# Two products of the second unit woven among the first unit's at the head of a Strassen-style gated layer

## The chip, the cores and the metric

The kernel runs on one core of a Trainium2 chip. The metric is the device time of one execution in microseconds (us); the time given is the median of the runs shown.

## The reference, cut to what matters

Causal attention, then a layer with a rational activation ("layer 1"), then a gated layer ("layer 2"), each on the output of the one before:

```python
x = attention(q, k, v)                       # 2 x 12 heads, 448 x 64 -> x is 896 x 768
h = x @ w_in                                 # 768 -> 2048
g = (a0 + a1*h + a2*h**2 + a3*h**3) / (1 + |b0|*|h| + |b1|*h**2 + 1e-6)
x = g @ w_out                                # 2048 -> 768
gate = 1 / (1 + exp(-(x @ w_gate)))          # 768 -> 1536
out = (gate * (x @ w_val)) @ w_out2          # 1536 -> 768, out is 896 x 768
```

The weights come as 64-bit floats and are unpacked on the chip. Every operand of a matrix product is kept as a pair hi, lo of two rounded numbers, and a product is three matmuls: hi by hi, hi by lo, lo by hi.

## The kernel before, in words

**Layer 1** works in four chunks (c = 0 to 3) of four 128-column tiles of `w_in`. The tokens come in two blocks (b = 0, 1); after the first chunk these are 384 and 512 tokens wide. For each chunk and block a stage "in" makes the tiles h and passes each through `rational` (lines 276 to 307: three ACT instructions L289 to L291, three of DVE L293 to L295, two of ACT L298 and L299, three of DVE L301 to L303, an ACT copy L305 to the hi half and a POOL subtraction L307 to the lo half), and a stage "out" multiplies by `w_out` in six column tiles e of four steps i each (matmuls L336 to L338). Each out tile is summed on DVE (L348); in the last chunk its result is rounded to xh (ACT L354) and xl (POOL L357).

**Layer 2** works in twelve units u. A unit makes the gate and the value product for 128 columns from seven products (`PRODUCTS`, a table of weights, activations and the PSUM accumulator A to D): p1 opens A, p6 opens B, p7 opens C, p5 opens D; p2, p4 and p3 add to A, C and D once these have been read. Each product is three steps of three matmuls (`product`, L475 to L477), nine in all. The sums of activations t1, t3, t2, t4 are made once, on DVE (`act_sum`, L448 to L454), rounded on ACT (L460) and their lo halves made on POOL, that of t3 on DVE (L464). `combine` (L480 to L512) reads the accumulators: "p1" is an ACT copy of A to x (L488), "u2" adds B to x (DVE L490), "u3" adds C and gives y (DVE L492), "c22" adds D to y (L494), "sg1" is the sigmoid of A (ACT L496), and so on to the halves gh and gl (ACT L510, POOL L512).

p2 can begin only after "p1" has read A, p4 only after "u3" has read C, and p3 only after "c22" has read D.

**The weights of a unit** come in two portions q (`weight2`): two DMAs each into a buffer `raw` (L402, two such buffers, shared with the portions of `w_out` and `w_out2`), two ACT instructions (L407, L409), one of DVE (L412). `weight_sums` makes s1 to s4 on DVE (L426 to L430) into the `raw` buffer of the second portion. Then each product's weights are copied to a slot's hi half by ACT (L436) and the lo half is subtracted on POOL (L440). There are ten slots; slots 8 and 9 lie in the second room of SBUF (room_b), the others in room_a. Unit u's product number n takes slot (7u + n) mod 10 and waits for the last matmul of the product that had the slot.

**The order** of each engine's instructions is fixed when the program is built. `stage_in`, `stage_out`, `unit_of_weights` and `stage_out2` write PE's order out by hand. Everything else is a job with an engine, a cost, its dependencies and a rank; `in_turn` (L35) takes on each engine, of the jobs that are ready by those costs, the one with the lowest rank. A rank is a place on PE's own line of costs plus an offset from the table `R`: "e" for DVE and POOL jobs of `combine`, "p1" for its ACT jobs, "ts", "th" and "tl" for the sums of activations, "w2" for unpacking a unit's weights, "wh" for its sums and halves, "sum" for what follows an out tile, in every chunk and in the output stage.

**The PSUM banks:** ring b has four banks and holds a unit's A to D (line 471); rings a and d have two each and hold the last six tiles of layer 1 and the tiles z of the output stage (`place`, line 925).

PE's order around the change is: the last out stage of layer 1; unit 0 as p1, p5, p2, p7, p6, p4, p3; units 1 and 2 each as p1, p6, p7, p5, p2, p4, p3; then the first group of the output stage (z, L529 to L531) over units 0 and 1, units 3 and 4, and so on.

Of the kernel before, what the change touches and what calls it, by code (L numbers as in the profile page):

```python
# [71 lines left out]
def tile_causal_attention__moe_rational__moe_glu(  # L72
# [349 lines left out]
    def weight_sums(u, k):  # L422
# [5 lines left out]
        else:  # L428
            nc.vector.tensor_tensor(a["s3"], a["a11"], a["a21"], op=ALU.subtract)
            nc.vector.tensor_tensor(a["s4"], a["a12"], a["s2"], op=ALU.subtract)  # L430

    def slot(u, name):
        return store["w"][(len(PRODUCTS) * u + list(PRODUCTS).index(name)) % NW]

    def weight_hi(u, name):
        nc.scalar.copy(slot(u, name)[0], halves[u, PRODUCTS[name][0]])  # L436
# [29 lines left out]
    def product(u, name, c):  # L466

        w, x, b, opens = PRODUCTS[name]
        if name == "p1" and c == 0:
            for k in "ABCD":  # L470
                unit_ps[u, k] = bank["b"].tile([P, 512], F32, tag="mm", name=f"u{u}_{k}")[:, :S]
        ps = unit_ps[u, b]
        (hi, lo), (bh, bl) = slot(u, name), act[x]
        begins, ends = opens and c == 0, c == KH - 1
        nc.tensor.matmul(ps, hi[:, c], bh[:, c], start=begins, stop=False, skip_group_check=True)  # L475
        nc.tensor.matmul(ps, hi[:, c], bl[:, c], start=False, stop=False, skip_group_check=True)  # L476
        nc.tensor.matmul(ps, lo[:, c], bh[:, c], start=False, stop=ends, skip_group_check=True)  # L477
# [239 lines left out]
    J = {}  # L717
# [12 lines left out]

    NG = len(GROUPS)
    LA = 2
    R = dict(last=0.0, rat0=-985.0, rat1=0.0, rl=4.0, s=-37.5, turn=-18.0, r=-8.0, row=-2.0, x=34.0, w=-3.0, max=-17.0, copy=-9.5, inv=1.0, xn=-0.5, rout=-4.0, exp=6.25, hi=18.0, lo=4.5, e=-8.0, p1=18.0, ts=-8.0, th=-7.0, tl=-6.5, wh=2.0, w2=-8.5, sum=-1.0)
    C = dict(w_at=11.0, row=0.1, o_at=37.98, o_step=3.0, w_step=5.5, s=0.28, p=0.1, x=0.15, max=0.08, exp=0.19, switch=0.05, stay=11.0, copy=0.0, wa=0.1, wd=0.26, xn=0.13, rat=0.16, inv=0.15)
    H = dict(PE=0.17, DVE=0.13, ACT=0.17, POOL=0.12, SP=0.03)
    MODES = {"s": "rows", "p": "rows", "x": "columns", "r": "rows"}
    EXP = (0.39, 0.48, 0.57, 0.67)
# [135 lines left out]
    def weights_in2(u):  # L873
# [10 lines left out]
        for k in range(2):  # L884
            deps = [("w2", u, 0, 3), ("w2", u, 1, 3)] + [("ws", u, 0)] * k
            job(("ws", u, k), "DVE", 1.1, deps, (("P", u, "p6", 0), R["wh"]), weight_sums, u, k)
        for i, name in enumerate(PRODUCTS):
            n = len(PRODUCTS) * u + i
            if n >= NW:
                free = [last_of((n - NW) // len(PRODUCTS), list(PRODUCTS)[(n - NW) % len(PRODUCTS)])]  # L890
# [36 lines left out]
    def place(key, read):  # L927

        after = key[:3] != ("in", 0, 0) and (key[:3] != ("in", 0, 1) or key[3] >= EARLY)
        n_tiles[after] += 1  # L930
        if key[:3] == ("out", NCH - 1, 1) or key[0] == "out2":
            n_tiles[2] += 1
            r = "ad"[n_tiles[2] // 2 % 2]
        else:
            r = "b" if after and (n_tiles[1] - 1) % 6 < 4 else "a"
        deps = freed_by(r, 4 if r == "b" else 2) + ["late"] * after
        freed[r].append([(*key, "after", read)])
        ring[key] = r
        return deps

# [70 lines left out]
        "gl2": ("POOL", 1.11, [], ["gh2"]),  # L1011
    }

    def unit_of_weights(u, order):

        nonlocal unit
        for name in order:
            deps = [("wl", u, name)]
            if not u and PRODUCTS[name][3]:
                deps += freed_by("b", 4 - "ABCD".index(PRODUCTS[name][2]))  # L1020
            deps += [("e", u, {"p2": "p1", "p4": "u3", "p3": "c22"}[name])] if name in ("p2", "p4", "p3") else []
            if u and PRODUCTS[name][3]:
                deps.append(("e", u - 1, {"A": "sg1", "B": "u2", "C": "pr1", "D": "pr2"}[PRODUCTS[name][2]]))
            for c in range(KH):
                x = PRODUCTS[name][1]
# [10 lines left out]
            for what, (engine, cost, after, others) in AFTER.items():  # L1036
# [2 lines left out]
                deps_e = [("P", u, n, KH - 1) for n in after] + [("e", u, o) for o in others]  # L1039
                if what == "p1" and u > 1:  # L1040
                    deps_e += [("e", u - 2, "c12"), ("e", u - 2, "gl1")]
                if what == "sg1":
                    deps_e += [("in", NCH - 1, 1, NF - 1, "after", 2)]
                    deps_e += [("e", u - 1, "c12")] if u else []
# [5 lines left out]
                if what == "gh2" and u < NG2 or what == "gh1" and u < NG2:  # L1050
                    deps_e.append(("out", NCH - 1, 1, KC - 1, "mm", NF - 1))
                job(("e", u, what), engine, cost, deps_e, at["end"] + R["p1" if engine == "ACT" else "e"], combine, u, what)

    def sums_of_x():

# [63 lines left out]
        _run(stage_out(*ins[n - 1]))  # L1119
    _run(stage_out(*ins[-1]))  # L1120
    sums_of_x()
    unit_of_weights(0, ("p1", "p5", "p2", "p7", "p6", "p4", "p3"))
    unit_of_weights(1, PRODUCTS)
    unit_of_weights(2, PRODUCTS)
    u = 3
    for group in range(len(GROUPS2)):
        _run(stage_out2(group))
        for _ in range(2):
            if u < NU and u < 2 * group + 5:
                unit_of_weights(u, PRODUCTS)  # L1130
                u += 1
    for j in J.values():
        if isinstance(j.rank, tuple):
            j.rank = at[j.rank[0]] + j.rank[1] if isinstance(j.rank[0], tuple) else at[j.rank]

    latest = {}
    for j in in_turn(J, {**H, "": 0.0}, C["switch"], C["stay"]):
# [59 lines left out]
```

## Time and profile before

| | |
|---|---|
| median of 3 runs | 577.6 us (577.32 to 578.62) |
| profiled execution, its own time | 580.54 us |
| its span | 577.5 us |
| time around the span | 3.04 us |
| PE busy | 559.4 us, 97% of the span, 3388 matmuls |
| DVE, ACT, POOL busy | 433.2, 383.4, 334.3 us |
| granted TensorE clock, mean | 0.997 |

A row of a timeline gives the start and the length of an instruction or of several alike (xN), and in brackets how long the engine had been idle and what ended that. Matmuls overlap: the pace is the distance of their starts, not their length. "SPq" is the queue from which the loads are issued.

### The profile page before, as it was taken

To read this page: it belongs to the slowest core of one execution; us is meant where nothing else is said; L and a number is where in the kernel's file an instruction comes from. 1 tells how busy PE (TensorE), PEld (TensorE's weight loads), DVE (VectorE), ACT (ScalarE), POOL (GpSimd) and SP (SyncE) were. 2 spreads that over 40 slices of the span, in tenths; PEclk is the share of its full clock that TensorE was granted. 3 is DMA by queue.
4 is the path that set the end of the run, shared out by engine and by line. 5 is a ranking of instruction groups with operands and counts; after the bars stand their busy time and mean duration, and the time that the engine had idled before them with its cause. 6 is when DMAs were issued, how large, how long until landed. Compare 5 with 4: busy or idle time off the path is not lost.

```text
span 577.5 us, 9390 instructions
## 1 busy us (share of the span) xinstructions
PE 559.4 (97%) x3388; PEld 486.0 (84%) x3388; DVE 433.2 (75%) x802; ACT 383.4 (66%) x767; POOL 334.3 (58%) x284
## 2 busy tenths in 40 slices
PE   7898999999999999999999989999999999999997
PEld 4455666699988988898888879999999999999996
DVE  5788899877758986899579877527876976757557
ACT  6799898788869494859285557577646466547210
POOL 1557544385377457445647987558647746665510
PEclk9899999999999999999999999999999999999999
DMA  8357540153154243304230103434244234432105
GB/s 278 106 186 239 178 137 18 33 187 102 63 171 158 65 155 102 117 0 132 88 111 0 56 0 110 165 110 149 71 165 140 69 120 165 126 129 76 53 0 192
DMA packets 35247, 65.29 MB, mean 113 GB/s; under 512 B 2369, under 2 KB 22593, under 8 KB 35201
## 3 DMA queue, kind: packets, MB, share of 16 engines
q1 hardware_dynamic: 35200, 64.70, 33.6%
q8 instruction: 26, 0.43, 0.3%
q14 instruction: 21, 0.16, 0.1%
HBM read 61.93 MB, written 2.75 MB: 112 GB/s over the span
## 4 chain that ended last, share of the span: by engine, by line
PE 83%; DVE 10%; POOL 2%; ACT 2%; DMA 1%; issue 1%; SPq 1%; DVEq 0%; POOLq 0%; ACTq 0%
PE h L274 7%; PE h L275 6%; PE h L276 6%; PE o L337 6%; PE o L338 6%; PE o L336 6%; PE z L529 5%; PE z L530 4%; PE z L531 4%; PE x L677 3%; PE s L595 3%; PE u_C L475 3%; PE u_C L477 3%; PE u_C L476 3%; PE u_A L475 2%; PE u_A L477 2%
## 5 line engine op out<-in xcount | busy, mean ns | idle before, releaser
L189 POOL TENSOR_TENSOR ol_out<-val_out,oh_out 128x768 fp32r<-128x768 f32 x28 | 55.2, 1971 | 10.9 <-ACT oh_out L187 9.5
L440 POOL TENSOR_TENSOR room_a<-val,room_a 128x384 fp32r<-128x384 f32 x30 | 32.5, 1091 | 42.3 <-ACT room_a L436 42.2
L529 PE MATMUL z<-oh_out,room_b 128*128 128x384 f32 (+2 forms) x168 | 56.6, 337 | 0.3 <-DVE y L539 0.3
L530 PE MATMUL z<-ol_out,room_b 128*128 128x384 f32 (+2 forms) x168 | 56.3, 335 | 0.0
L531 PE MATMUL z<-oh_out,room_b 128*128 128x384 f32 (+2 forms) x168 | 56.2, 335 | 0.0
L539 DVE TENSOR_TENSOR y<-y,z 128x384 f32<-128x384 f32 (+1 forms) x84 | 43.8, 550 | 12.6 <-PE z L531 12.4
L617 ACT ACTIVATE e<-e,sc 120x224 f32<-120x224 f32 (+3 forms) x96 | 49.8, 524 | 4.6 <-DVE sc L603 4.5
L440 POOL TENSOR_TENSOR room_a<-raw,room_a 128x384 fp32r<-128x384 f32 x38 | 45.8, 1221 | 8.4 <-ACT room_a L436 8.4
L603 DVE CUSTOM_DVE_ANT_0 e<-s,mask 120x224 f32<-120x224 f32 (+3 forms) x96 | 38.0, 444 | 14.1 <-PE s L595 14.0
L177 DVE SCALAR_TENSOR_TENSOR val_out<-raw_out 128x768 uint32<-128x768 uint32 x28 | 35.7, 1276 | 16.6 <-ACT raw_out L174 10.3
L307 POOL TENSOR_TENSOR room_a<-t_h,room_a 128x384 fp32r<-128x384 f32 (+1 forms) x16 | 17.9, 1121 | 48.8 <-ACT room_a L305 48.6
L307 POOL TENSOR_TENSOR room_b<-t_h,room_b 128x512 fp32r<-128x512 f32 (+1 forms) x16 | 21.7, 1357 | 36.5 <-ACT room_b L305 36.5
L595 PE MATMUL s<-qk 64*120 64x224 f32 (+3 forms) x192 | 32.3, 437 | 6.2 <-DVE sc L603 6.2
L337 PE MATMUL o<-room_b,oh_out 128*128 128x512 f32 (+1 forms) x96 | 37.0, 386 | 1.0 <-POOL room_b L307 1.0
L274 PE MATMUL h<-xh,room_a 128*128 128x448 f32 (+2 forms) x96 | 36.9, 384 | 0.7 <-DVE t_h L295 0.7
L338 PE MATMUL o<-room_b,ol_out 128*128 128x512 f32 (+1 forms) x96 | 36.9, 385 | 0.0
L336 PE MATMUL o<-room_b,oh_out 128*128 128x512 f32 (+1 forms) x96 | 36.8, 384 | 0.0
L289 ACT ACTIVATE z_h<-h 128x384 f32<-128x384 f32 (+2 forms) x32 | 17.5, 548 | 26.5 <-PE h L276 26.5
L275 PE MATMUL h<-xl,room_a 128*128 128x448 f32 (+2 forms) x96 | 35.0, 364 | 0.0
L276 PE MATMUL h<-xh,room_a 128*128 128x448 f32 (+2 forms) x96 | 34.9, 363 | 0.0
L275 PE MATMUL h<-xl,room_b 128*128 128x384 f32 (+1 forms) x96 | 34.7, 362 | 0.0
L412 DVE SCALAR_TENSOR_TENSOR val<-raw 128x768 uint32<-128x768 uint32 x24 | 24.3, 1013 | 13.9 <-ACT raw L409 13.8
(179 smaller groups left out, 1866.8 us busy)
## 6 DMA issues: line engine op xcount, KB each, us to landing
raw_out<-in_moe_w_out_dram SPq DMA_DIRECT2D x28, 768.0 KB, 4.2
raw_in<-in_moe_w_in_dram SPq DMA_DIRECT2D x16, 768.0 KB, 4.9
raw<-in_moe_w_gate_dram SPq DMA_DIRECT2D x24, 384.0 KB, 3.3
raw<-in_moe_w_val_dram SPq DMA_DIRECT2D x24, 384.0 KB, 3.9
qk<-in_qk_dram SPq DMA_DIRECT2D x12, 464.0 KB, 5.5
v<-in_v_dram SPq DMA_DIRECT2D x12, 224.0 KB, 3.4
out_dram<-y SPq DMA_DIRECT2D x14, 192.0 KB, 2.4
a_sb<-in_moe_a_dram SPq DMA_DIRECT2D x1, 2.0 KB, 6.8
```

The lines of the kernel that those rows point to most:

```text
L189: nc.gpsimd.tensor_tensor(lo, vf, hi, op=ALU.subtract)
L274: nc.tensor.matmul(ps, hi[:, c, fs], xh[:, c, bs], start=(c == 0), stop=False)
L275: nc.tensor.matmul(ps, hi[:, c, fs], xl[:, c, bs], start=False, stop=False)
L276: nc.tensor.matmul(ps, lo[:, c, fs], xh[:, c, bs], start=False, stop=(c == KC - 1))
L336: nc.tensor.matmul(ps, hi[:, es], gh, start=(i == 0), stop=False)
L337: nc.tensor.matmul(ps, hi[:, es], gl, start=False, stop=False)
L338: nc.tensor.matmul(ps, lo[:, es], gh, start=False, stop=(i == NF - 1))
L440: nc.gpsimd.tensor_tensor(lo, halves[u, PRODUCTS[name][0]], hi, op=ALU.subtract)
L529: nc.tensor.matmul(ps, gh[:, ms], hi[:, ns], start=(u == us[0]), stop=False)
L530: nc.tensor.matmul(ps, gh[:, ms], lo[:, ns], start=False, stop=False)
L531: nc.tensor.matmul(ps, gl[:, ms], hi[:, ns], start=False, stop=(u == us[-1]))
L617: nc.scalar.activation(e, e, AF.Exp, bias=d["sc"][:, t, j : j + 1], scale=-1.0, accum_out=d["sum"][:, t, j : j + 1])
```

## The change

Unit 0 and unit 1 are issued as one list in which p1 of unit 1 stands between p5 and p2 of unit 0, and p2 of unit 1 between p6 and p4 of unit 0. The accumulator A of unit 1 takes a bank of ring a or d; when p6 of unit 1 begins, four tiles of ring b are taken as before and the one for A stays unused. Unit 1's order and its slots follow the new tuple AHEAD. Six offsets of `R` change, and one job (the second DVE step of `rational` for the third tile of layer 1's last stage "in") gets a rank lower by 2.5.

```diff
+    AHEAD = ("p1", "p2", "p6", "p7", "p5", "p4", "p3")
+    def turns(u):
+        return AHEAD if u == 1 else list(PRODUCTS)
     def slot(u, name):
-        return store["w"][(len(PRODUCTS) * u + list(PRODUCTS).index(name)) % NW]
+        return store["w"][(len(PRODUCTS) * u + turns(u).index(name)) % NW]
...
-        if name == "p1" and c == 0:
+        if u == 1 and name == "p1" and c == 0:
+            unit_ps[u, "A"] = psum_tile(("unit", 1), "u1_A")
+        elif name == ("p1" if u != 1 else "p6") and c == 0:
             for k in "ABCD":
-                unit_ps[u, k] = bank["b"].tile([P, 512], F32, tag="mm", name=f"u{u}_{k}")[:, :S]
+                t = bank["b"].tile([P, 512], F32, tag="mm", name=f"u{u}_b{k}")[:, :S]
+                unit_ps.setdefault((u, k), t)
...
-    R = dict(... e=-8.0, p1=18.0, ts=-8.0, th=-7.0, tl=-6.5, wh=2.0, w2=-8.5, sum=-1.0)
+    R = dict(... e=7.5, p1=18.0, ts=-5.5, th=-0.5, tl=-1.0, wh=2.0, w2=-11.5, sum=7.0)
+    NUDGE = {'in 3 1 2 after 3': -2.5}
...
-        if key[:3] == ("out", NCH - 1, 1) or key[0] == "out2":
+        if key[:3] == ("out", NCH - 1, 1) or key[0] in ("out2", "unit"):
             n_tiles[2] += 1
             r = "ad"[n_tiles[2] // 2 % 2]
...
-        freed[r].append([(*key, "after", read)])
+        freed[r].append([(*key, "after", read) if key[0] != "unit" else ("e", key[1], "sg1")])
...
-    def unit_of_weights(u, order):
+    def units_of_weights(order):
...
-            if u and PRODUCTS[name][3]:
+            if (u, name) == (1, "p1"):
+                deps += place(("unit", 1), None)
+            elif u and PRODUCTS[name][3]:
...
                 if what == "p1" and u > 1:
                     deps_e += [("e", u - 2, "c12"), ("e", u - 2, "gl1")]
+                    deps_e += [("e", 1, "c12")] if u == 2 else []
...
-    unit_of_weights(0, ("p1", "p5", "p2", "p7", "p6", "p4", "p3"))
-    unit_of_weights(1, PRODUCTS)
-    unit_of_weights(2, PRODUCTS)
+    units_of_weights([(0, "p1"), (0, "p5"), (1, "p1"), (0, "p2"), (0, "p7"), (0, "p6"), (1, "p2"),
+        (0, "p4"), (0, "p3"), (1, "p6"), (1, "p7"), (1, "p5"), (1, "p4"), (1, "p3")])
+    unit_of_weights(2)
...
-    for j in J.values():
+    for key, j in J.items():
...
+        j.rank += NUDGE.get(" ".join(str(k) for k in key), 0.0)
```

## Rows read from the trace of the kernel before

**Rows 1.** The page: busy time of the engines, share of the span, instructions.

```profile
PE 559.4 (97%) x3388; PEld 486.0 (84%) x3388; DVE 433.2 (75%) x802; ACT 383.4 (66%) x767; POOL 334.3 (58%) x284
```

**Rows 2.** PE's waits, whole span: total us, times, longest.

```profile
PE u_C L475 <- DVE y L492: 1.5, 1, 1.5
...
PE o L337 <- POOL room_b L307: 1.0, 1, 1.0
PE u_A L475 <- ACT x L488: 0.8, 1, 0.8
```

**Rows 3.** PE's timeline from unit 0's first matmul to unit 2's p6.

```profile
328.50 0.36 PE L475 MATMUL u_A<-xh,room_a 128*128 128x448 f32 x1
...
331.95 0.36 PE L477 MATMUL u_D<-xh,room_a 128*128 128x448 f32 x1
333.12 0.47 PE L475 MATMUL u_A<-xh,room_a 128*128 128x448 f32 x1 [0.81 <-ACT x L488]
...
338.59 0.37 PE L477 MATMUL u_B<-room_a 128*128 128x448 f32 x1
340.48 0.44 PE L475 MATMUL u_C<-room_b,room_a 128*128 128x448 f32 x1 [1.53 <-DVE y L492]
...
357.01 0.37 PE L475 MATMUL u_A<-xh,room_a 128*128 128x448 f32 x1
...
359.24 0.36 PE L477 MATMUL u_B<-room_a 128*128 128x448 f32 x1
```

**Rows 4.** ACT's timeline, from 332 to 357 us.

```profile
332.54 0.53 ACT L488 COPY x<-u_A 128x448 f32<-128x448 f32 x1
...
351.05 0.91 ACT L407 ACTIVATE raw<-raw 128x768 f32<-128x768 f32 x1
...
355.62 1.33 ACT L436 CAST room_a<-raw 128x384 fp32r<-128x384 f32 x3
```

**Rows 5.** DVE's timeline, instructions from 302 to 354 us.

```profile
302.77 0.55 DVE L348 TENSOR_TENSOR y<-y,o 128x384 f32<-128x384 f32 x1 [1.52 <-PE o L338]
...
313.17 1.51 DVE L426 TENSOR_TENSOR raw<-val,val 128x384 f32<-128x384 f32 x1
...
335.60 2.64 DVE L454 TENSOR_TENSOR y<-y 128x448 f32<-128x448 f32 x3
339.06 0.62 DVE L490 TENSOR_TENSOR x<-x,u_B 128x448 f32<-128x448 f32 x1 [0.82 <-PE u_B L477]
339.71 0.62 DVE L492 TENSOR_TENSOR y<-x,u_C 128x448 f32<-128x448 f32 x1
...
353.82 0.56 DVE L426 TENSOR_TENSOR raw<-val,val 128x384 f32<-128x384 f32 x1
```

**Rows 6.** POOL's timeline, instructions from 308 to 361 us.

```profile
308.07 1.02 POOL L440 TENSOR_TENSOR room_a<-val,room_a 128x384 fp32r<-128x384 f32 x1 [0.61 <-ACT room_a L436]
...
312.35 1.91 POOL L307 TENSOR_TENSOR room_b<-t_h,room_b 128x512 fp32r<-128x512 f32 x1
...
337.85 2.49 POOL L464 TENSOR_TENSOR room_b<-y,room_b 128x448 fp32r<-128x448 f32 x2 [1.16 <-ACT room_b L460]
340.69 1.17 POOL L464 TENSOR_TENSOR room_b<-y,room_b 128x448 fp32r<-128x448 f32 x1 [0.35 <-ACT room_b L460]
...
344.74 1.02 POOL L440 TENSOR_TENSOR room_a<-raw,room_a 128x384 fp32r<-128x384 f32 x1
345.71 1.85 POOL L189 TENSOR_TENSOR ol_out<-val_out,oh_out 128x768 fp32r<-128x768 f32 x1
...
354.59 2.56 POOL L440 TENSOR_TENSOR room_b<-val,room_b 128x384 fp32r<-128x384 f32 x2 [2.34 <-ACT room_b L436]
357.11 4.02 POOL L440 TENSOR_TENSOR room_a<-raw,room_a 128x384 fp32r<-128x384 f32 x3
```

**Rows 7.** The load queue's timeline: unit 2's second portion.

```profile
345.78 0.37 SPq L402 DMA_DIRECT2D raw<-in_moe_w_gate_dram  x1
```

**Rows 8.** One stretch of layer 1: busy time (instructions) of PE, PEld, DVE, ACT, POOL; clock; DMA.

```profile
150.00:300.00 150.00, 150.00 (x742) 134.50 (x741) 118.67 (x186) 105.42 (x180) 84.16 (x63) 1.00 0.32 105
```

More of the change, by code (lines that the diff above doesn't have):

```diff
@@ L732, in tile_causal_attention__moe_rational__moe_glu @@
     LA = 2
-    R = dict(last=0.0, rat0=-985.0, rat1=0.0, rl=4.0, s=-37.5, turn=-18.0, r=-8.0, row=-2.0, x=34.0, w=-3.0, max=-17.0, copy=-9.5, inv=1.0, xn=-0.5, rout=-4.0, exp=6.25, hi=18.0, lo=4.5, e=-8.0, p1=18.0, ts=-8.0, th=-7.0, tl=-6.5, wh=2.0, w2=-8.5, sum=-1.0)
+    R = dict(last=0.0, rat0=-985.0, rat1=0.0, rl=4.0, s=-37.5, turn=-18.0, r=-8.0, row=-2.0, x=34.0, w=-3.0, max=-17.0, copy=-9.5, inv=1.0, xn=-0.5, rout=-4.0, exp=6.25, hi=18.0, lo=4.5, e=7.5, p1=18.0, ts=-5.5, th=-0.5, tl=-1.0, wh=2.0, w2=-11.5, sum=7.0)
     C = dict(w_at=11.0, row=0.1, o_at=37.98, o_step=3.0, w_step=5.5, s=0.28, p=0.1, x=0.15, max=0.08, exp=0.19, switch=0.05, stay=11.0, copy=0.0, wa=0.1, wd=0.26, xn=0.13, rat=0.16, inv=0.15)
+    NUDGE = {'in 3 1 2 after 3': -2.5}
     H = dict(PE=0.17, DVE=0.13, ACT=0.17, POOL=0.12, SP=0.03)
@@ L886, in weights_in2 @@
             job(("ws", u, k), "DVE", 1.1, deps, (("P", u, "p6", 0), R["wh"]), weight_sums, u, k)
-        for i, name in enumerate(PRODUCTS):
+        for i, name in enumerate(turns(u)):
             n = len(PRODUCTS) * u + i
             if n >= NW:
-                free = [last_of((n - NW) // len(PRODUCTS), list(PRODUCTS)[(n - NW) % len(PRODUCTS)])]
+                before, k = divmod(n - NW, len(PRODUCTS))
+                free = [last_of(before, turns(before)[k])]
             else:
@@ L1012, in tile_causal_attention__moe_rational__moe_glu @@
     }
-    def unit_of_weights(u, order):
+    def units_of_weights(order):
         nonlocal unit
-        for name in order:
+        for u, name in order:
             deps = [("wl", u, name)]
@@ L1052, in unit_of_weights @@
                 job(("e", u, what), engine, cost, deps_e, at["end"] + R["p1" if engine == "ACT" else "e"], combine, u, what)
+    def unit_of_weights(u):
+        units_of_weights([(u, name) for name in PRODUCTS])
     def sums_of_x():
@@ L1121, in tile_causal_attention__moe_rational__moe_glu @@
     sums_of_x()
-    unit_of_weights(0, ("p1", "p5", "p2", "p7", "p6", "p4", "p3"))
-    unit_of_weights(1, PRODUCTS)
-    unit_of_weights(2, PRODUCTS)
+    units_of_weights(
+        [
+            (0, "p1"),
+            (0, "p5"),
+            (1, "p1"),
+            (0, "p2"),
+            (0, "p7"),
+            (0, "p6"),
+            (1, "p2"),
+            (0, "p4"),
+            (0, "p3"),
+            (1, "p6"),
+            (1, "p7"),
+            (1, "p5"),
+            (1, "p4"),
+            (1, "p3"),
+        ]
+    )
+    unit_of_weights(2)
     u = 3
@@ L1129, in tile_causal_attention__moe_rational__moe_glu @@
             if u < NU and u < 2 * group + 5:
-                unit_of_weights(u, PRODUCTS)
+                unit_of_weights(u)
                 u += 1
-    for j in J.values():
+    for key, j in J.items():
         if isinstance(j.rank, tuple):
             j.rank = at[j.rank[0]] + j.rank[1] if isinstance(j.rank[0], tuple) else at[j.rank]
+        j.rank += NUDGE.get(" ".join(str(k) for k in key), 0.0)
     latest = {}
```

## The prediction

> **What bounds the kernel now.** I read the page first: PE is busy for 97% of the span, DVE for 75% [rows 1]. The time is therefore PE's matmuls plus PE's waits, so the second view is the list of PE's waits. Outside attention, which no part of the change reaches, three stand out: 1.5 us before p4 of unit 0, 1.0 us in layer 1's last out stage, 0.8 us before p2 of unit 0 [rows 2]. The change is placed at the first and the last of these.
>
> The third view is PE's timeline there [rows 3]. Unit 0 starts at 328.50 us. After p1 and p5 the last matmul starts at 331.95, and p2 only at 333.12: it waits for the ACT copy of A to x, which runs 332.54 to 333.07 [rows 4]. After p6 the last matmul starts at 338.59, and p4 only at 340.48: it waits for DVE's u2 and u3, 339.06 to 340.33 [rows 3, 5]. From there PE runs without a break to unit 2's first matmul at 357.01.
>
> The pace without waits: from 340.48 to 357.01 lie nine products (p4 and p3 of unit 0, seven of unit 1), 16.53 us, so 1.84 us for each.
>
> **The two covered waits.** No matmul is added or removed; nine go in front of p2 and nine in front of p4. Fourteen products at 1.84 us are 25.7 us. Unit 2 would then begin at 328.50 + 25.7 = 354.2 instead of 357.01: 2.8 us are to be had (more than the 0.81 and 1.53 in the brackets, because the matmuls behind a wait and the three products between the waits start at a slightly slower pace).
>
> Is the cover long enough? Before p2 it is ample: p1 of unit 1 runs from 332.15 to 333.98, and the copy ended at 333.07. Before p4 it is close: from the last start of p6 to that of p4 the old kernel took 1.89 us, of which one pace (0.20) would have passed anyway, so 1.69 are to be covered by 1.84. It holds by 0.15 us, if DVE turns to u2 and u3 as promptly as before. Each takes 0.62 [rows 5]; one other DVE job put between would cost 0.6 to 1.6 less the 0.15. Offset "e" rises from -8 to 7.5, so those jobs lose urgency; but DVE had nothing left when p6 ended (idle 0.82 before L490), so I take nothing for it.
>
> **Are the moved products' weights there?** p1 of unit 1 has its halves by 309.1: the subtraction of its lo half, 1.02 us at 308.07, ended an idle stretch of POOL before which ACT had made the hi half [rows 6]. That is 23 us before its new place. p2 of unit 1 moves from slot 1 to slot 8, which was free early; its source, like that of s1 and s2, is unpacked before the sums begin at 313.17 [rows 5]. Its two halves (one ACT, one POOL instruction) change places with those of p7, which moves from slot 9 to slot 0. The work on ACT and POOL stays the same in number: cost nothing, covered by the 26 us between 313 and p2's new place at 339.5. The x copy of unit 1 (0.53 on ACT) only comes earlier. That of unit 2 now waits for unit 1's c12 too, but p2 of unit 2 follows three products, 5.5 us, after p1: nothing. The bank of unit 1's A comes from a layer 1 tile three before the last, so p1 of unit 1 waits for that tile's sum; two out tiles and two products lie between, nothing. The unused tile of ring b costs no instruction.
>
> **Unit 2 comes 2.8 us earlier: are its weights?** This is what is late next. Its p6 needs s2, made in the `raw` buffer of its second portion. That load is issued at 345.78, the moment POOL finishes the last lo half that reads unit 1's sums (344.74 + 1.02) [rows 6, 7]. From it follow L407 at 351.05, the DVE sums at 353.82, the hi copies at 355.62 and the lo halves from 357.11, three in 4.02 us, the first done at about 358.45 [rows 4 to 6]. p6's first matmul with a lo half starts at 359.24 [rows 3]: a slack of 0.8 us. 2.8 us earlier it wants its lo at 356.4. If the chain from the load keeps its times, a new wait of 2.0 us appears. But the chain is loose: after the two DVE sums that make s2 (353.82 and 0.56 each, to 354.94) one hi copy (1.33/3 = 0.44) and one lo half (1.02) could follow directly and end at 356.4 to 356.6, a wait of 0.2; instead POOL spent 354.59 to 357.15 on two halves in room_b that p2 and p4 want much later [rows 4 to 6]. A load issued half a microsecond earlier takes that away too. A gain is excluded, since no wait stands there now. So the price lies between 0 and 2.0; I take the middle, 1.0, for nothing in the rows says which copies will stand in front, while offset "w2", lower by 3, favours the unpacking. Behind p6 the halves come every 1.34 us against 1.84 of PE, so no second wait.
>
> **The out stage's wait of 1.0 us.** PE waited for a lo half by POOL at 312.35, which ended a chain that began when DVE sat idle for 1.52 us before an out-tile sum at 302.77, though `rational` work stood behind it in the same queue [rows 5, 6]. "sum" goes from -1 to 7 and one `rational` step is lowered by 2.5: out-tile sums give way. At best all of the 1.0 goes. At worst, since the sums now come later everywhere, a wait of the same size comes up elsewhere: +1.0. PE was busy without a break from 150 to 300 us [rows 8], so the sums had room there; I put it nearer the gain: 0.5 saved.
>
> **Sum.** -2.8 + 1.0 - 0.5 = -2.3 us on the span of 577.5, so 575.2, and 578.2 for the profiled execution's own time of 580.54. The runs' median is 577.6, 2.9 below that one execution; the difference of 2.3 is carried over: 575.3.
>
> **The rivals.**
>
> *The wait moves to unit 2 in full.* For it: the rows of unit 2 as they stand, with a release of the buffer that hangs on POOL, which paused only 1.16 and 0.35 us in the ten before it [rows 6]. Against: p7 and p3 of unit 1 get their slots after p1 and p5 of unit 0, so two of the three late halves can go into POOL's pause of 1.16 us [rows 6]. Then -2.8 + 2.0, with nothing from the out stage: -0.8, 576.8.
>
> *DVE slows when POOL's pause is filled.* L426 took 1.51 us at 313.17 and 0.56 at 353.82, for the same shape; POOL was in a subtraction beside the first and idle beside the second [rows 5, 6]. The three t4 sums, 2.64 us at 335.60, run partly in POOL's pause of 1.16. If a lo half fills that pause and each sum takes about 1.5, they take 4.5, and t4's last lo half comes 1.9 later than 341.86, at 343.7. p4 of unit 0 starts at 341.4 and wants it seven matmuls on, at 342.8: a wait of 0.9. Unit 2 then comes 1.9 earlier; its price is 0.5 if its weights are packed half as tightly as they could be, and 3.0 if the lo halves behind t4's, and so the load, are late by 1.9 too. The sum is between -2.8 + 0.9 + 0.5 - 0.5 = -1.9 and +0.6: 575.7 to 578.2, about 577.0. The Trainium skill's page "SBUF — State Buffer", section "Who interferes with whom", states this as a rule: a DVE instruction with two SBUF inputs contends with a GpSimd instruction that reads SBUF. By that rule the t4 sums (two SBUF inputs) would be slowed, and u2 and u3 (one input from PSUM) would not; the trace agrees with the 0.62 of both.
>
> *Slower: the release of `raw` slips.* p5 of unit 1 also reads a sum, and moves from slot 0, free at 330.5, to slot 1, free when p6 of unit 0 ends, about 339.5. If its lo half, or p3's, is queued behind the w_out2 subtraction (1.85) [rows 6] and two gl halves (estimate: 1.02 x 448/384, 1.2 each), the load starts 4.2 us later, at 350; p6 of unit 2 then waits 2.0 + 4.2 = 6.2, and the sum is -2.8 + 6.2 - 0.5 = +2.9: 580.5. It decides from a release at 347.1 on (1.3 later than now), where 2.0 + 1.3 uses up the 2.8 and the 0.5. For it: the order is rewritten by ranks that know costs and not these rows. Against: "e" at 7.5 makes the gl halves less urgent.
>
> *The change does not do what it says*, that is PE waits as long at p2 and p4: only if the x copy or u3 moves by more than 0.9 or 0.15 us. I count the second under the forecast's spread.
>
> **Chances.** Forecast 0.55; wait moved to unit 2 in full 0.20; DVE slowed 0.10; release slipped 0.15. 0.2%, about what a measurement of this kernel can tell from no change, is 1.15 us: faster means below 576.45, slower above 578.75. The forecast and 0.03 of the DVE case are faster, 0.58; the second case and 0.06 of the DVE case are within, 0.26; the slip and the last 0.01 are slower, 0.16. Range: best case -2.8 - 1.0 = 573.8, to 573.6 with the runs' 0.3 below their median; upwards past the second and third case (576.8, 578.2) and the small slips to 578.6, so that most of the slip case is left out, and little else.
>
> **What would show it.** Right: no PE wait before p2 and p4 of unit 0, nine matmuls of u_A from unit 1 in each place, unit 2's first matmul some 25.7 us after unit 0's. The 1.0 shows in a PE wait at u_B of unit 2 on POOL L440; zero there makes the time 574.3. Wrong: a wait at u_B above 2.8, a second load for unit 2 issued later than 18 us after unit 0's start, or new waits in the out stages of layer 1 because of late sums.

## The result and the profile after

The change makes the kernel slower: 582.09 us (median of 11 runs, 580.43 to 585.03) against 578.62 for the kernel before in the same set of runs, ratio 1.0063 [1.0044, 1.0082], about 3.6 us. A second set gave 1.0038 [1.0018, 1.0058], about 2.2 us. The forecast was 575.3 in a range of 573.6 to 578.6.

The page of the changed kernel, the row of [rows 1]:

```profile
PE 561.7 (97%) x3388; PEld 486.5 (84%) x3388; DVE 436.6 (75%) x802; ACT 384.7 (66%) x767; POOL 336.6 (58%) x284
```

The number of instructions is the same on every engine. So the difference is not more instructions but waits, and a slightly slower pace behind them. PE's waits in layer 2, in the place of [rows 2] (total us, times, longest):

```profile
PE u_bB L485 <- POOL room_a L445: 1.8, 1, 1.8
PE u_bC L484 <- DVE room_b L469: 1.4, 1, 1.4
...
PE u_bB L483 <- ACT z L504: 0.9, 1, 0.9
```

All three rows of [rows 2] are gone, and three new ones stand there. PE's timeline of the same stretch as [rows 3] (the product is now L483 to L485, the p1 copy L496, the hi copy of weights L441, their lo half L445):

```profile
327.12 0.36 PE L483 MATMUL u_bA<-xh,room_a 128*128 128x448 f32 x1
...
332.59 0.36 PE L483 MATMUL u_bA<-xh,room_a 128*128 128x448 f32 x1
...
337.63 0.47 PE L484 MATMUL u_bC<-room_b,room_a 128*128 128x448 f32 x1 [1.36 <-DVE room_b L469]
...
354.86 0.36 PE L483 MATMUL u_bA<-xh,room_a 128*128 128x448 f32 x1
...
357.02 0.47 PE L483 MATMUL u_bB<-room_a 128*128 128x448 f32 x1 [0.17 <-ACT room_a L441]
...
359.47 0.47 PE L485 MATMUL u_bB<-room_a 128*128 128x448 f32 x1 [1.77 <-POOL room_a L445]
```

p2 of unit 0 (332.59) waits for nothing, and neither does p4: the weave does what it says. But p7, which did not wait before, waits 1.36 us; and p6 of unit 2 (357.02 and 359.47) waits 1.9 us.

The wait in p7 is on DVE's queue:

```profile
329.38 3.07 DVE L469 TENSOR_TENSOR room_b<-y,room_a 128x448 fp32r<-128x448 f32 x2
332.37 0.74 DVE L348 TENSOR_TENSOR y<-y,o 128x64 f32<-128x64 f32 x2
333.14 0.81 DVE L455 TENSOR_TENSOR y<-y 128x448 f32<-128x448 f32 x1
...
334.53 1.57 DVE L459 TENSOR_TENSOR y<-y 128x448 f32<-128x448 f32 x1
336.03 1.55 DVE L469 TENSOR_TENSOR room_b<-y,room_a 128x448 fp32r<-128x448 f32 x1
337.50 2.10 DVE L459 TENSOR_TENSOR y<-y 128x448 f32<-128x448 f32 x2
```

The last out tile's sum (L348) stands behind two lo halves of t3, 3.07 us ("sum", which ranks it, went from -1 to 7). The third sum of t3 (L455) needs that tile. Its lo half (L469) then stands behind a sum of t4 as well (L459, 1.57 us) and ends at 337.58, when p7 goes on. In the kernel before the out tile's sum came 1.9 us sooner, and the last lo half of t3 (L464) ahead of every sum of t4 (L454, at 335.60 in [rows 5]):

```profile
330.45 0.74 DVE L348 TENSOR_TENSOR y<-y,o 128x64 f32<-128x64 f32 x2
...
334.10 1.58 DVE L464 TENSOR_TENSOR room_b<-y,room_a 128x448 fp32r<-128x448 f32 x1
```

The wait at p6 of unit 2 is the chain from the load, as in [rows 4, 6, 7], from the timelines of the load queue, ACT and POOL:

```profile
345.94 0.37 SPq L402 DMA_DIRECT2D raw<-in_moe_w_gate_dram  x1
...
352.05 0.91 ACT L407 ACTIVATE raw<-raw 128x768 f32<-128x768 f32 x1 [1.25 <-DMA raw<-in_moe_w_val_dram]
...
355.42 2.72 POOL L445 TENSOR_TENSOR room_b<-val,room_b 128x384 fp32r<-128x384 f32 x2 [3.18 <-ACT room_b L441]
358.10 4.00 POOL L445 TENSOR_TENSOR room_a<-raw,room_a 128x384 fp32r<-128x384 f32 x3
```

The load is issued at 345.94 (before 345.78), the two halves in room_b still go first, and the first lo half of the next three ends at about 359.4 (358.45 before). PE came 2.15 us sooner and used none of it.

The issue is not what made the chain late: L407 begins 1.0 us later than before because the second half of the load took longer. These are the rows of that half (its size, and the us from issue to landing) and of the next load, a portion of `w_out2`, on the same queue; first after, then before:

```profile
raw<-in_moe_w_val_dram SPq DMA_DIRECT2D x1, 384.0 KB, 5.6
350.28 0.34 SPq L162 DMA_DIRECT2D raw_out<-in_moe_w_out_dram  x1
```

```profile
raw<-in_moe_w_val_dram SPq DMA_DIRECT2D x1, 384.0 KB, 3.9
350.63 0.34 SPq L162 DMA_DIRECT2D raw_out<-in_moe_w_out_dram  x1
```

In before the load had landed by 350.1, and L407 stood behind another conversion on ACT; in after it landed at 352.0, 1.7 us after the next load had been issued. So about 1 us of the 1.94 us at unit 2 is the load's own. It repeats: 5.3 us in after_again, 4.0 in before_again.

The rest of the loss lies behind the stretch that was changed. Rows of PE, ACT, DVE and the load queue, first of the changed kernel, then (DVE and the queue) of the kernel before:

```profile
424.61 0.50 PE L537 MATMUL z<-oh_out,room_b 128*128 128x512 f32 x1 [0.62 <-DVE y L547]
...
441.78 0.47 PE L483 MATMUL u_bB<-room_a 128*128 128x448 f32 x1 [0.91 <-ACT z L504]
...
440.77 0.51 ACT L441 CAST room_b<-raw 128x384 fp32r<-128x384 f32 x1 [0.46 <-DVE raw L430]
441.19 0.54 ACT L504 ACTIVATE z<-u_bA 128x448 f32<-128x448 f32 x1
...
422.29 1.80 DVE L177 SCALAR_TENSOR_TENSOR val_out<-raw_out 128x768 uint32<-128x768 uint32 x1
...
424.11 0.37 SPq L402 DMA_DIRECT2D raw<-in_moe_w_gate_dram  x1
```

```profile
418.47 1.81 DVE L177 SCALAR_TENSOR_TENSOR val_out<-raw_out 128x768 uint32<-128x768 uint32 x1
...
420.31 0.37 SPq L402 DMA_DIRECT2D raw<-in_moe_w_gate_dram  x1
```

L177 unpacks weights of the output stage and frees the buffer into which unit 6 is loaded. It comes 3.8 us later in DVE's new order (3.5 counted from the first z), and the load with it. The sums of z tiles (L547) stand behind it, and z waits 0.62 us. What ends PE's wait at p6 of unit 6 is the sigmoid of unit 5 (L504): on ACT it stands behind the hi halves made from the late load. Why p6 needs that sigmoid, no view shows. These two places make up most of the 2.4 us.

**The ledger.** The stages are cut by the starts of PE's first matmuls: of the last out stage, of unit 0, of the first z group, and the last matmul of all. Lengths in us, from one profile each; the ratio is of the timed runs.

| kernel | out stage | unit 0 to z | z to end | sum | ratio |
|---|---|---|---|---|---|
| before | 30.11 | 41.28 | 203.24 | 274.6 | |
| after | 28.87 | 43.00 | 205.62 | 277.5 | 1.0063 [1.0044, 1.0082] |
| weave_only | 29.92 | 43.82 | 204.30 | 278.0 | 1.0052 [1.0015, 1.0089] |
| ranks_only | 28.86 | 47.58 | 203.02 | 279.5 | 1.0072 [1.0049, 1.0096] |
| sum_back | 30.12 | 43.24 | 205.20 | 278.6 | 1.0057 [1.0038, 1.0077] |
| e_sum_back | 30.12 | 43.68 | 203.57 | 277.4 | 1.005 [1.003, 1.007] |
| p6_first | 28.87 | 42.00 | 206.15 | 277.0 | 1.0056 [1.0036, 1.0075] |
| release_early | 28.86 | 45.24 | 205.02 | 279.1 | 1.0101 [1.0082, 1.012] |
| both_moved | 28.86 | 45.46 | 207.87 | 282.2 | 1.0152 [1.0126, 1.0178] |
| all_moved | 28.86 | 41.17 | 206.75 | 276.8 | 1.0088 [1.0062, 1.0113] |
| weave_held | 30.12 | 41.39 | 202.69 | 274.2 | 1.0027 [1.001, 1.0043] |
| weave_held_chain | 30.10 | 41.03 | 203.45 | 274.6 | 0.9993 [0.9979, 1.0007] |
| weave_held_all | 28.86 | 41.50 | 204.27 | 274.6 | 1.0004 [0.998, 1.0028] |
| held_out | 28.87 | 43.45 | 202.90 | 275.2 | 1.0035 [1.0018, 1.0052] |
| held_hand | 28.87 | 41.86 | 204.00 | 274.7 | 0.9992 [0.9978, 1.0006] |
| held_hand_dve | 28.87 | 40.93 | 203.22 | 273.0 | 0.9993 [0.9975, 1.0012] |
| held_dve | 30.12 | 41.30 | 202.92 | 274.3 | 1.0003 [0.9988, 1.0018] |
| before_again | 30.12 | 41.29 | 203.26 | 274.7 | 1.0001 [0.9984, 1.0018] |
| after_again | 28.87 | 42.89 | 205.19 | 277.0 | 1.0038 [1.0018, 1.0058] |
| held_hand_dve_again | 28.87 | 41.10 | 203.11 | 273.1 | 0.9973 [0.9953, 0.9993] |

Of the change, then: -1.24 in the out stage, +1.72 from unit 0 to z, +2.38 from there on, together +2.9 us.

### The profile page after: what moved, and what is told of

Same layout as the page of the kernel before. It is cut to its first block, busy times and chain, and to the rows that moved or that the text cites. A ratio compares the mean times of both kernels' runs of the same rounds, so it can differ in the third digit from the quotient of the medians.

```text
span 580.6 us, 9385 instructions
## 1 busy us (share of the span) xinstructions
PE 561.7 (97%) x3388; PEld 486.5 (84%) x3388; DVE 436.6 (75%) x802; ACT 384.7 (66%) x767; POOL 336.6 (58%) x284
## 4 chain that ended last, share of the span: by engine, by line
PE 79%; DVE 11%; DMA 3%; ACT 3%; issue 2%; POOL 1%; SPq 1%; DVEq 0%; ACTq 0%; POOLq 0%
PE h L274 7%; PE o L338 6%; PE o L337 6%; PE o L336 6%; PE h L275 6%; PE h L276 6%; PE z L537 4%; PE z L539 4%; PE z L538 4%; PE x L685 3%; PE s L603 3%; DVE e L611 2%; PE u_bD L483 2%; PE u_bD L484 2%; PE u_bC L483 2%; PE u_bC L484 2%
## 5 line engine op out<-in xcount | busy, mean ns | idle before, releaser
L445 POOL TENSOR_TENSOR room_a<-val,room_a 128x384 fp32r<-128x384 f32 x29 | 31.8, 1107 | 40.7 <-ACT room_a L441 40.0
L445 POOL TENSOR_TENSOR room_a<-raw,room_a 128x384 fp32r<-128x384 f32 x39 | 48.3, 1256 | 8.3 <-ACT room_a L441 8.3
L547 DVE TENSOR_TENSOR y<-y,z 128x384 f32<-128x384 f32 (+1 forms) x84 | 43.3, 550 | 9.2 <-PE z L539 9.1
L177 DVE SCALAR_TENSOR_TENSOR val_out<-raw_out 128x768 uint32<-128x768 uint32 x28 | 37.0, 1321 | 16.9 <-ACT raw_out L174 10.8
L412 DVE SCALAR_TENSOR_TENSOR val<-raw 128x768 uint32<-128x768 uint32 x24 | 23.6, 984 | 20.0 <-ACT raw L409 13.3
L407 ACT ACTIVATE raw<-raw 128x768 f32<-128x768 f32 x24 | 21.9, 914 | 22.7 <-DMA raw<-in_moe_w_val_dram 22.7
```

The source lines that it names most:

```text
L445: nc.gpsimd.tensor_tensor(lo, halves[u, PRODUCTS[name][0]], hi, op=ALU.subtract)
```

## Experiments: the two halves of the change, and single places

```diff
 weave_only (after):      R and NUDGE as before
 ranks_only (before):     R and NUDGE as after
 sum_back (after):        sum=7.0 -> -1.0
 e_sum_back (after):      sum=7.0 -> -1.0, e=7.5 -> -8.0
```

> The changed kernel with the six offsets of before and no nudge: only the order of the products, unit 1's slots and its PSUM bank are new. Theory (the loss after unit 2 comes from the new offsets, the weave itself is only used up at unit 2's p6): PE has no wait before p2 and p4 of unit 0, a wait of about 2 us at p6 of unit 2, the old 1.0 us in layer 1's last out stage, and after unit 2 the same distances as before; time 0.3 to 1.0 us under the kernel before. Rival (the weave itself delays the weights of the later units): 2 to 3.5 us slower than the kernel before, with the new waits in the output stage's second group and at p6 of unit 6 still there.

> The kernel before with the six new offsets and the nudge, products in the old order. Theory (offsets cost): the wait in the last out stage goes (-1.0), the two waits of unit 0 stay or grow because of later sums (0 to +1.4), the later waits in the output stage and at unit 6 appear (+2.5); sum 1.5 to 3 us slower than before. Rival (the weave costs): 1 us faster to equal.

> The changed kernel with only the offset sum back at -1. Theory (late out-tile sums are what makes the new waits): the 1.4 us before t3's third step in p7 of unit 0 and the waits in the output stage go, the 1.0 in layer 1's last out stage may come back; 1 to 3 us faster than the changed kernel, within 1 us of the kernel before. Rival (offset e or w2 makes them): within 0.7 us of the changed kernel.

> The changed kernel with the offsets sum and e back at -1 and -8; ts, th, tl, w2 and the nudge stay new. Theory (sum and e together make the later loss): as weave_only within 0.6 us, at or up to 1 us under the kernel before. Rival (w2 and the t offsets make it): within 1 us of the changed kernel, 2 to 3.5 us slower than before.

Neither half is faster. **The weave alone** removes the waits at p2 and p4 and gets one of 3.09 us in unit 1 instead, which nobody had priced (PE, DVE, ACT, and the busy time of a stretch: PE, PEld, DVE, ACT, POOL, clock, DMA):

```profile
356.49 0.66 PE L483 MATMUL u_bD<-xh,room_a 128*128 128x448 f32 x1 [3.09 <-DVE y L502]
...
354.94 0.96 DVE L412 SCALAR_TENSOR_TENSOR val<-raw 128x768 uint32<-128x768 uint32 x1 [4.30 <-ACT raw L409]
355.82 0.61 DVE L502 TENSOR_TENSOR y<-y,u_bD 128x448 f32<-128x448 f32 x1
...
353.21 0.88 ACT L407 ACTIVATE raw<-raw 128x768 f32<-128x768 f32 x1 [3.08 <-DMA raw<-in_moe_w_val_dram]
...
356.40:360.00 3.60, 3.51 (x10) 3.13 (x11) 3.32 (x5) 2.61 (x6) 3.60 (x4) 0.53 0.00 0
```

p3 of unit 1 needs c22 (L502), and c22 stands in DVE's queue behind an unpacking step (L412) that waits 4.30 us for a load. In the old order of unit 1, p2 lay between p5 and p4 and gave the sums behind p5 and p7 a product more of time. The weave takes that product away: cover was moved from unit 1 to unit 0, not made. That is not all of the 3.09: the planner also put c22 behind L412 (before, it came ahead of it), and that load took 5.7 us to land, 1.8 more than in before. After the wait the granted clock is 0.53 for 3.6 us.

**The offsets alone** end the out stage's wait (28.86) but leave the two waits of unit 0 (1.08 at p2, 1.37 at p4) and bring a third of 2.64 us, for the rounding of the last out tile to xh on ACT, late through the late sum (L348 at 334.06); and the clock is at 1.2 GHz (0.50) behind it:

```profile
334.93 0.74 PE L475 MATMUL u_A<-xh,room_a 128*128 128x448 f32 x1 [2.64 <-ACT xh L354]
...
334.90:339.00 4.10, 4.05 (x10) 3.25 (x11) 4.10 (x4) 3.77 (x6) 4.04 (x4) 0.50 0.00 0
```

**sum_back** shows that "sum" is the term of the out stage: with -1 the 0.96 us wait is back (30.12), the one in p7 falls to 0.60, and a 1.96 us wait for c22 of unit 1 comes up. In sum_back a sum of t4 (1.57 us) still stands ahead of t3's last lo half, so the offsets "ts", "th" and "tl" have a part in it: with all offsets of before, in weave_only, p7 doesn't wait. From z on nothing was won, against the expectation. **e_sum_back** takes 1.6 us off the time from z on, compared with sum_back. So "e" at 7.5 makes most of that loss in the woven kernel. The offsets alone (203.02) don't make it, and the weave with the offsets of before still loses 1.1 (204.30).

```diff
 p6_first (after):       wh of unit 2's p2 and p4 depend on wl of its p6
 release_early (after):  ranks of wh and wl of unit 1's p7, p3, p5 lower by 20; its p4 behind p5 and p3
 both_moved (after):     both
 all_moved (after):      both, and the steps of the last out tile's sum lower by 8
```

> The changed kernel; the weights' halves of p2 and p4 of unit 2 are made to wait until the lo half of p6 of unit 2 is done. Theory (PE's 1.8 us wait at p6 of unit 2 is the end of the chain from the load of unit 2's second portion, and two halves that nobody needs yet stand in it on POOL): that wait falls from 1.8 to 0.2 to 0.6, the stretch from unit 0's first matmul to the first output tile from 43.0 to about 41.5; 1 to 1.8 us faster than the changed kernel. Rival (the wait has another last cause, or the time is lost again behind it): the stretch shrinks by less than 0.5 or the total by less than 0.5.

> The changed kernel; on POOL the lo halves of p7, p3 and p5 of unit 1, which read the buffer of the sums, are taken ahead by their ranks, and that of p4, which does not, comes behind them. Theory (the same chain begins with the release of that buffer, 345.9 in the changed kernel): the load of unit 2's second portion is issued 1.5 to 2 us earlier, the wait at p6 of unit 2 falls to 0 to 0.5, 1.3 to 2 us faster than the changed kernel. Rival (the chain is held by ACT's and DVE's order, not by the load): the load comes earlier, the wait stays above 1.3.

> Both edits together. Theory: no wait at p6 of unit 2; the stretch from unit 0's first matmul to the first output tile falls from 43.0 to 40.5 to 41.2; about 2 us faster than the changed kernel, still slower than before by 1 to 2 for the later waits (output stage, unit 6). Rival: new waits of the same size elsewhere in units 0 to 2, the stretch above 42.

> Both edits, and the sum of the last tile of layer 1's last out stage, with what follows it, gets a rank lower by 8, which undoes the new offset sum for that tile alone. Theory (PE's 1.4 us wait in p7 of unit 0 is this sum standing behind two lo halves of t3 on DVE): that wait goes too, the stretch is 39 to 40 us against 41.3 of the kernel before, and the time is at or up to 1.5 us under the kernel before unless the later waits of 2.4 stay in full (then 0 to 1 above). Rival: DVE is simply full there, the wait in p7 stays at 1 us or more.

p6_first does what it should at its place: the waits there are 0.42 and 0.57 instead of 0.17 and 1.77, and the stretch is 1.0 us shorter. But a wait of 0.88 appears at p6 of unit 4, z to the end is 206.15, and the time is no better. release_early fails at its own place: the load is issued 47.5 us behind the start of the last out stage (47.7 in after), hardly earlier, and the copy of A in unit 0 (L496) comes on ACT only at 336.30, behind other conversions:

```profile
336.88 0.63 PE L483 MATMUL u_bA<-xh,room_a 128*128 128x448 f32 x1 [4.24 <-ACT x L496]
```

both_moved has the same wait of 4.24. all_moved has the load at 46.2 us and the shortest stretch of the eight (41.17), 1.4 us ahead of before at z, and gives it back from z on (206.75, waits of 0.77 and 1.35 at p6 of unit 4). In each of these kernels a few ranks or dependencies were changed and the planner made a new order for every queue; so a single cause can't be read off them.

## Experiments: the old order held, and only named instructions moved

For these the loop that emits the jobs takes them in the order of the kernel before, read from a list, and only the named jobs have another place. The weave needs the halves of unit 1's weights in other slots, so those move with it.

```diff
-    for j in in_turn(J, {**H, "": 0.0}, C["switch"], C["stay"]):
+    for j in in_place(J):
 weave_held:        the woven products and their slots; unit 1's copy of A and its u3 move too
 weave_held_chain:  also wh, wl of unit 1's p5 and p3 ahead of p4's; of unit 2's p6 and p5 ahead of p2's and p4's
 weave_held_all:    also the sums of the out tiles 2 to 4 (block 0) behind one step of rational fewer
 held_out (before): the sums alone
```

> Edit: the kernel before with the two products of unit 1 woven in among unit 0's (in the output ring's bank), and every other instruction left in the order of before on its queue; no planner, no offsets of the changed kernel. Theory (the weave's two waits, 2.8 us, are really taken away, unit 2's second portion takes 1 to 2 us of that back because its load comes no earlier, and what the changed kernel loses behind that comes from the planner's new order on the queues): no wait at p2 and p4 of unit 0, a wait of 1.5 to 2.5 us at p6 of unit 2 on POOL, unit 0 to z0 40 to 41 us (before 41.3), z0 to the last matmul 203.0 to 203.6 (before 203.2, changed 205.6), the 1.0 us wait of the output stage ahead stays; 0.3 to 1.5 us under before. Rival (a product taken out of unit 1's tail always costs as much cover there as it gives in unit 0): a wait of 2 us or more in unit 1 at its raw's arrival or at y, 42 us or more from unit 0 to z0, at or above before.

> Edit: as the held weave, with the conversions that free raw in unit 1 ahead of unit 1's p4, and unit 2's p6 conversions ahead of those of its p2 and p4. Theory: the load of unit 2's second portion starts about 1.5 us earlier and its last conversion ends earlier by 1 to 2 us, so the wait at p6 of unit 2 shrinks to under 0.8 us and unit 0 to z0 is 38.7 to 39.5 us; 1.5 to 3 us under before. Rival (the wait moves to what was put back: p4 of unit 1 or p2 or p4 of unit 2): a wait of 1 us or more on POOL or ACT at one of these, unit 0 to z0 no shorter than in the held weave.

> Edit: as the one before, and in the output stage before unit 0 the sums that end the wait of 1.0 us (L307 on POOL) are put one place earlier, behind the multiplications of one tile less. Theory: that wait goes, so a further 0.7 to 1.2 us under the last one, 2 to 4 us under before. Rival (the sum moved forward delays DVE's or POOL's part in unit 0): a new wait of 1 us or more in the first products of unit 0, no gain over the last one.

> Edit: the kernel before with the move in the output stage alone, no product woven. Theory: its 1.0 us wait goes and 0.5 to 1.2 us stay gained if nothing behind is late; the waits of 1.5 and 1.3 us at p2 and p4 of unit 0 stay. Rival: those two waits grow by as much as was gained, since what they wait for does not come earlier; then within 0.3 us of before.

Most of the loss from z on is gone (202.69 to 204.27, before 203.24, after 205.62): it came from the new order, as the theory had it. The gain did not come. In weave_held, unit 0 to z takes 41.39 us, the 2.8 being replaced by 1.24 at p4 of unit 1 (u3) and 1.17 at p6 of unit 2. weave_held_chain takes the second away (its load is issued 47.2 us behind the start of the out stage, 48.2 in weave_held), and the first stays: 41.03, where 38.7 to 39.5 were expected. **held_out** was the surprise. The out stage is 1.24 us shorter and the next wait is longer by 2.2 (0.81 before). Two rows of weave_held, then two of held_out:

```profile
352.62 0.47 PE L597 MATMUL u_bC<-room_b,room_a 128*128 128x448 f32 x1 [1.24 <-DVE y L614]
359.93 0.47 PE L599 MATMUL u_bB<-room_a 128*128 128x448 f32 x1 [1.17 <-POOL room_a L559]
```

```profile
326.20 0.36 PE L589 MATMUL u_A<-xh,room_a 128*128 128x448 f32 x1
...
333.00 0.47 PE L589 MATMUL u_A<-xh,room_a 128*128 128x448 f32 x1 [2.99 <-ACT x L602]
```

So what unit 0 waits for, the copy of A in ACT's held order, does not come earlier when PE does. With both edits, weave_held_all, out stage and stretch together are 70.36 us against 71.39 before and 72.32 in held_out: the weave covers what held_out loses, and z to the end gives the 1.0 back (204.27).

```diff
 held_hand:      weave_held_all, and earlier on their queues: copy of A (unit 0), u3, the second sigmoid
                 and product (unit 1), the first sigmoid (unit 3), one xh of the last out tile
 held_hand_dve:  held_hand, and
-        nc.gpsimd.tensor_tensor(lo, ...)
+        (nc.vector if (u, name) in ((1, "p5"), (1, "p3")) else nc.gpsimd).tensor_tensor(lo, ...)
 held_dve:       the same two lo halves on DVE, in the kernel before
```

> Edit: as weave_held_all, with four places changed by hand: the copy of A in unit 0 ahead of a conversion, u3 of unit 1 ahead of the next portion's unpacking, the sigmoid and the product of unit 1's second half ahead of the output weights' unpacking, the sigmoid of unit 3 ahead of two conversions. Theory (POOL's queue and the load behind it set when unit 2's second portion is there, not PE's order): the waits of 1.2 us (A's copy), 0.2 us (u3) and 0.5 us (unit 2's p5) go, the one at p6 of unit 2 grows from 0.2 to 1 to 2 us, the load stays at 345.5 to 345.9, z0 is no more than 0.7 us earlier, and the time is within 0.8 us of weave_held_all. Rival (the four places were the whole rest): p6 waits under 0.5 us, unit 0 to z0 is 39.3 to 39.8 us, 1.5 to 2 us under before.

> Edit: as held_hand, and the lo halves of unit 1's p5 and p3 computed by DVE instead of POOL, behind unit 0's sum c22. Theory: raw is free 1 to 2 us earlier (load at 343.7 to 344.7), p6 of unit 2 waits 1 us or less, unit 0 to z0 is 38.7 to 39.5 us, and the time is 1.5 to 3 us under before. Rival (DVE beside POOL takes 1.4 us or more for one and is itself late: c21 and the gates behind it): the load no earlier than 345.2, or a new wait of 1 us or more on DVE in unit 0 or 1, no gain over held_hand.

> Edit: the kernel before, not woven, with the lo halves of unit 1's p5 and p3 on DVE (and the conversions and halves of p4 behind those of p5 and p3). Theory (before, unit 2's p6 finds its weights there, so an earlier load buys nothing): the load is 1 to 2 us earlier, the waits of 0.8 and 1.5 us at p2 and p4 of unit 0 stay, and the time is within 0.5 us of before. Rival (the load sets later stages too): 0.8 us or more under before.

held_hand bears the theory out in the sum and not at the place. The waits named are gone (u3's 0.24 stays), the load is still issued at 345.50 (47.4 us behind the start of the out stage, as in weave_held_all), and the time is that of weave_held_all; but PE is held up by POOL's lo halves already in unit 0 (0.44 and 0.43), so only 0.8 of the expected 1 to 2 us is left for p6 and p7 of unit 2. With two lo halves off POOL:

```profile
333.44 0.47 PE L600 MATMUL u_bA<-xl,room_a 128*128 128x448 f32 x1 [0.44 <-POOL xl L472]
341.59 0.47 PE L600 MATMUL u_bC<-room_b,room_a 128*128 128x448 f32 x1 [0.43 <-POOL room_b L585]
350.01 0.47 PE L599 MATMUL u_bC<-room_b,room_a 128*128 128x448 f32 x1 [0.46 <-DVE y L616]
...
343.38 0.37 SPq L517 DMA_DIRECT2D raw<-in_moe_w_gate_dram  x1
```

Counted from the start of the out stage the load comes 1.1 us earlier (46.3), and nothing waits at unit 2 any more; z to the end is back at 203.2. Part of this may be the load itself: its second half took 5.7 us to land in held_hand and 3.8 here. What is left in the stretch, 40.93 us, are three waits on lo halves and u3, so the 38.7 to 39.5 expected were not reached. held_dve has the early load too (343.81, 45.3 behind the start of the out stage) and gains nothing, as expected: there p6 had its weights in time.

## Experiments: do the stages repeat?

> Edit: none, the kernel before once more, as a control. If the stages of a profile repeat: output stage before unit 0 30.1 us, unit 0 to the first z group 41.3, from there to the last matmul 203.2, each within 0.3, and a ratio of 1.000 within 0.002. If they do not: 0.5 us or more off in one of them.

> Edit: none, the changed kernel once more. If the stages repeat: output stage 28.9 us, unit 0 to the first z group 43.0, from there to the last matmul 205.6, each within 0.4, a ratio of 1.004 to 1.008. If they do not, the loss of 1.7 and 2.4 us is not the same in the second profile.

> Edit: none, held_hand_dve once more. If its 1.6 us are real: output stage to the first z group 69.8 us again (before 71.4), and 0.3 to 1.5 us under before, since the timed runs of the first time spread over 4 us. Rival: the same stages, and again no difference of the times over 0.2%; then what was gained there is lost in stretches that differ from run to run.

They do, nearly: before within 0.02 us in each stage, after within 0.43 (0.4 was expected), held_hand_dve within 0.2. held_hand_dve is 1.6 us shorter than before in both profiles. Its timed runs say 0.9993 [0.9975, 1.0012] and 0.9973 [0.9953, 0.9993]: a gain of 0.4 us by the one and 1.6 by the other, clear of no change in the second only. No other version has an interval below 1, but that it is the best is not shown: weave_held_chain stands at 0.9993 too.

## Why the prediction was wrong

The forecast was 2.3 us saved; the stages came out 2.9 us longer. The out stage did 0.7 better than forecast, the stretch from unit 0 to z 3.5 worse (+1.7 in place of -1.8), and everything behind z, for which no term stood in the sum, cost 2.4. The step that failed most is thus one that was left out, the price of the new offsets behind the head of layer 2; in unit 0 to z it is a wait that the sum lacked and one that it took at half.

**The two covered waits: right at their place.** -2.8 was the price of two waits, and both are gone. But unit 2 began 27.74 us behind unit 0 (354.86 - 327.12), not 25.7: the wait of 1.36 in p7, and the slower pace around it, were not in the sum. The step on offset "e" ("I take nothing for it") looked at the wrong offset and the wrong neighbour. "sum" put an out-tile sum of DVE behind 3.07 us of t3's lo halves, the offsets of the t sums put a sum of t4 in front of the last of them, and the term for "sum" was looked for in the out stages alone.

**The price at unit 2: mis-sized.** It was put between 0 and 2.0 and taken at 1.0. It was 1.94 (0.17 + 1.77), the top, as the first rival has it ("the wait moves to unit 2 in full"). The tight packing (one hi copy and one lo half at once) didn't occur; POOL did the two halves in room_b first, as before: the row of before had already shown the order. p6_first, which changes that order, halves the wait. But the full 2.0 was reached partly by luck: unit 2 came 2.0 us earlier instead of 2.8 (counted from the last out stage), and the chain did not keep its times, since the load took 1.7 us longer to land. The prediction read L407 at 351.05 as following the load; in before the load had landed 0.9 us ahead of it.

**The out stage: mis-sized the other way.** -0.5 was taken; the stage is 1.24 shorter. held_out shows what that is worth: by itself +0.9 us up to z, since unit 0's copy of A comes at its own time.

**What no step priced.** (1) Everything from z on: +2.4 of the 2.9 us. Offsets are read by every unit, and the prediction costed them at the head of layer 2 alone. (2) The cover taken out of unit 1: p2's place between p5 and p4. In after itself it costs nothing, in weave_only a part of 3.09, in weave_held 1.24. The sentence that p2 "moves" priced its weights and its copy, not the gap it left.

**The rivals.** The slower one (the release of raw slips) did not occur: the load is at 345.94. Its +2.9 is the loss of the stages to the digit, but by coincidence. The sign set for it, a load later than 18 us behind unit 0's start, did come (18.8 us; 17.3 in before), because unit 0 begins earlier and the load does not. That of a slower DVE occurred in part: the three t4 sums took 3.67 us (1.57 and 2.10) instead of 2.64 [rows 5], but p4 comes later by the wait in p7 and found their lo halves there. The causes of the measured loss, other than unit 2's, stand in no case.

**The reason under it.** In the stretch from unit 0's start to z, an earlier PE does not bring the end forward by itself. Counted from the start of the last out stage, the load of unit 2's second portion is issued at 47.4 us in before, 47.7 in after, 47.4 in weave_held_all and 47.4 in held_hand, although unit 0 begins 1.2 us earlier in the last three; it is later still in weave_held (48.2) and held_out (48.3). In each of these it is issued as POOL ends the last lo half that reads unit 1's sums. Taking two lo halves off POOL moved it to 46.3, and only that version is 1.6 us shorter up to the end. So much is shown. Up to z, weave_held_all had 1.0 of it already and all_moved, with the load at 46.2, 1.4; why their later stages lose 1.0 and 3.5 us, and those of held_hand_dve nothing, was not traced. Whether a better order of the later units gives more was not tried, nor was a further buffer for the loads.

## What to carry to other kernels

A wait of PE is worth its length only if what comes next is earlier too: before covering it, find the engine whose queue sets the next buffer (here POOL, seen by a load whose time did not move), look what that load will meet on its queue, and price the gap that a moved product leaves as well as the one it fills. Where a planner makes all queues anew from a few offsets, change the order by name and hold the rest; the eight edits through offsets and dependencies lie 2.2 to 7.6 us above before in the sum of the stages, the seven in a held order between -1.6 and +0.6.

## What the runs showed of the hardware

The granted clock moved single times by as much as most edits did. In the profile of before it is 0.66 in one stretch of attention, and 1.00 in held_hand_dve_again, in the same stretch (busy time of PE, PEld, DVE, ACT, POOL; clock; DMA; PE had been busy for 3.18 and 3.43 of the five us ahead). The last out stage begins at 298.4 in the one and at 296.7 in the other, and up to it every engine has the same instructions in the same order in both:

```profile
15.00:20.00 5.00, 5.00 (x41) 2.56 (x40) 2.19 (x8) 2.84 (x7) 0.00 (x0) 0.66 0.06 22
```

```profile
15.00:20.00 5.00, 4.77 (x61) 2.90 (x60) 3.81 (x14) 3.96 (x10) 1.05 (x2) 1.00 0.17 42
```

Up to there that holds for all twenty profiles, and they divide in the same way: eleven show a lower clock between 12 and 28 us and begin that stage at 298.1 to 300.6, nine show none there and begin it at 296.7 to 297.6.

Among executions whose mean clock is 0.999 or 1.000 the median spans are 576.4 us before (71 of the 130 whose clock is known), 579.7 after (14 of 23) and 575.4 for held_hand_dve (9 of 24): +3.3 and -1.0 without the clock. In the same comparison weave_held_all has 575.4 (5 of 12) and weave_held_chain 575.6 (6 of 12), as little as held_hand_dve. Of weave_only and ranks_only none of the 14 is among them; each profile has a wait of 2.6 to 3.1 us and then a clock at or near 0.5, the level of 1.2 GHz. The waits of 1.95 us in e_sum_back and 1.96 in sum_back were followed by 0.72 over the next 6 us, the 4.24 us in release_early and both_moved by 0.72 and 0.53; the 1.77 us in after by 1.00, and so was the 2.99 us in the profile of held_out, of whose 12 timed executions 10 are below 0.999. The Trainium skill, page "TensorE: Matmul & The Clock Gate", section "Part 1: The HAM clock gate", has the clock at half when TensorE has been idle. The traces agree behind six of these waits (3.09, 2.64, 1.95, 1.96 and twice 4.24 us); behind held_out's 2.99 and after's 1.77 they show no fall.

In these profiles a load took longer when the next one followed closely. The 384 KB of `w_val` of unit 2 landed 5.3 to 5.7 us after their issue in the six profiles in which the 768 KB of `w_out2` were issued 2.2 to 3.9 us behind them. Of the fourteen profiles in which these followed after 4.3 us or more, thirteen have 3.7 to 4.7 us and one (held_hand) 5.7. In before the `w_out2` load followed after 4.4 us, in after 3.9: it is issued as the unpacking step L412 ends, on DVE (350.60 and 350.25). No run was made to test this by itself.
